# Attention with wide key chunks: three chunks of 128 keys and a shared rest of 64 instead of four chunks of 112, from unit 18 on

## The chip, the cores and the metric

The kernel runs on one core of one Trainium2 chip. The metric is the device time of one execution in microseconds (us). A NeuronCore has a matrix engine (TensorE, PE in the profile, its weight loads PEld), a vector engine (VectorE, DVE), a scalar engine (ScalarE, ACT), GpSimd (POOL), and SyncE (SP), which here issues the stores and the transposes by DMA. Each engine works through its own list of instructions in order and waits on semaphores where it needs another's result.

## The reference

Attention over 8 batches and 12 heads, 448 tokens each, head size 64, and behind it a two-layer network with a leaky ReLU:

```python
scores = scale * np.matmul(q, k.transpose(0, 1, 3, 2))
attn = softmax(scores)                       # over the 448 keys
attn_out = np.matmul(attn, v)                # (8, 12, 448, 64)
x = attn_out.transpose(0, 2, 1, 3).reshape(3584, 768)
h = x @ w_in                                 # 768 -> 2048
g = np.maximum(0.01 * h, h)
return (g @ w_out).astype(np.float32)        # 2048 -> 768
```

Inputs and output are float32; the products inside the kernel run in bfloat16. The kernel takes no maximum off the scores: it exponentiates the scaled scores directly, and divides by the sum afterwards.

## The kernel before, in words

**Units.** A unit is two heads of one batch: 48 units, six to a batch. For each unit q, k and v are loaded by DMA (converted to bfloat16 on the way), and copied by POOL into `qkb` (q and k side by side) and into `v_sb`, which holds a column of ones behind each head's 64 columns. q and k are then turned so that the head dimension lies on the partitions: `qkT`, with head 0 on partitions 0 to 63 and head 1 on 64 to 127. The first units are turned by PE, those from unit 15 on by a DMA transpose that SP issues (`dma_transposes`, L257).

**Scores.** The 448 keys are cut into four chunks of 112 (`SC`). A chunk is two matmuls of 448 columns (`scores`, L284), one for each head, each contracting the 64 rows of its half; they go to one PSUM slot of two banks. ACT exponentiates the slot in one instruction of 112 x 896 (`expo`, L296) into `e_sb`. Three such slots rotate. In the main part chunks come in bursts of three (`burst`, L819): six matmuls in a row, then three exponentials. A burst so covers three quarters of a unit.

**Rows.** When all of a unit's exponentials are there, `rows` (L790) multiplies them by v: for each of two heads, four groups of 112 queries and four key chunks one matmul of 65 columns, 32 in all; the 65th column is the sum of the exponentials. DVE takes the reciprocal of the sums and multiplies (L805, L806) into an x tile. `x_transposes` has SP turn the x tile by DMA into `xT`; for four units PE does it. The x tiles rotate over three buffers: the multiply of a unit must wait until the transpose of the unit three before has read its buffer.

**The network.** The 3584 tokens are cut into seven ranges (0, 640, 1152, 1664, 2176, 2688, 3072, 3584), numbered 0 to 6. For each range there are two stages. `hidden` computes the first layer in products of six matmuls (L489), in two chains with two PSUM banks each; ACT copies or DVE adds (L504, L516, L519) must empty a bank before the chain comes back to it. `second` computes the second layer from blocks of products of eight matmuls of 384 columns (L561), whose results DVE gathers into the tile o, which SP stores. Products are combined in a scheme that needs seven block products instead of eight, hence the many sums on DVE.

**The order of the work.** Everything is written in one program order, from which each engine takes its own instructions. Bursts and rows are put between the matmuls of `second` by `place` (L878), which keeps a small model of time (when PE is, when ACT will be through, when a slot will be free) and places a burst or the rows of a unit only when the model says that PE would not wait. `plan` (L875) says how many bursts go into each `second` stage: 9, 8, 8, 8, 8, 5, 0. In `hidden` there are no bursts, as two of the three slots serve the chains; rows of units that are ready are put in at every fourth step (L1001). At regular steps `advance` (L768) issues the loads (POOL), the casts (POOL) and the qkT transposes (SP) of later units. SP's list thus holds stores, qkT transposes and xT transposes in one order, and each waits for those ahead of it to be issued.

In the profile's time: `second` of range 0 runs from about 74 to 104 us, and then `hidden` and `second` of ranges 1 to 6 follow, with `hidden` from 104, 152.5, 201.5, 250, 298.5 and 341 us for ranges 1, 2, 3, 4, 5 and 6.

Of the kernel before, what the change touches and what calls it, by code (L numbers as in the profile page):

```python
# [16 lines left out]
def kernel(  # L17
# [9 lines left out]
    nc = tc.nc  # L27
# [9 lines left out]
    NW = DM // 2  # L37
    NU = B * HP
    scale = 1.0 / float(D) ** 0.5

# [8 lines left out]
    w_pool = ctx.enter_context(tc.tile_pool(name="weights", bufs=1))  # L49
    ld_pool = ctx.enter_context(tc.tile_pool(name="ld", bufs=2))  # L50
    cast_pool = ctx.enter_context(tc.tile_pool(name="cast", bufs=1))
# [30 lines left out]
    PL = D + 2  # L82
    v_sb = [v_pool.tile([SC, 2, NSC, VL], BF16, name=f"v{i}") for i in range(NV)]

    NE = 3
    EL = 2 * NSC * S
    e_sb = [exp_pool.tile([SC, EL + P - SC], BF16, name=f"e{i}") for i in range(NE)]


    NQ = 4  # L90
    QL = 2 * S
    qkT = [qk_pool.tile([P, QL + P - SC], BF16, name=f"qkT{i}") for i in range(NQ)]

# [25 lines left out]
    qk_sb = {}  # L119
    qkb = [cast_pool.tile([SC, 2, NSC, 2, D], BF16, name=f"qkb{i}") for i in range(4)]  # L120

# [3 lines left out]
    for t, n in ((h_mix, 2), (w_in_mix, 9), (w_mix, 9)):  # L125
        t = t.rearrange("p x k n -> p (x k n)")
        for j in range(n):
            rooms.append(t[:SC, ts(j, 4 * NSC * D)].bitcast(F32).rearrange("p (h so d) -> p h so d", h=2, so=NSC))

    def room(x):  # L130

        return rooms.pop(0) if rooms else ld_pool.tile([SC, 2, NSC, D], F32, name="f" + "qkv"[x])

    def half(t, i=None):

        t = t.rearrange("p h so d -> p (h so d)").bitcast(BF16)
        t = t.rearrange("p (u h so d) -> p u h so d", u=2, h=2, so=NSC)
        return t if i is None else t[:, i]

    def load_soft(u, n, which):  # L140
        b, hp = divmod(u, HP)
        for x in which:
            t = room(x)
            nc.gpsimd.dma_start(
                out=half(t)[:, :n].rearrange("p u h so d -> p (u h) (so d)"),
                in_=(q, k, v)[x][b, 2 * hp:2 * hp + 2 * n].rearrange(
                    "h (p so) d -> p h (so d)", so=NSC),
            )
            for i in range(n):
                raw.setdefault(u + i, {})[x] = half(t, i)  # L150

    def load_one(u, x, queue):
        b, hp = divmod(u, HP)
        t = room(x)
# [10 lines left out]
    def cast(u, parts=(0, 1, 2), by=nc.gpsimd.tensor_copy):  # L165
        if u >= NU:
            return
        for x in parts:
            f = raw[u].pop(x)
            if x < 2 and u not in qk_sb:  # L170
                qk_sb[u] = qkb[u % len(qkb)]
            t, n = (qk_sb[u][:, x], D) if x < 2 else (v_sb[u % NV], D)
            if f.dtype == BF16 and by == nc.gpsimd.tensor_copy:
                t, f, n = t.bitcast(F32), f.bitcast(F32), D // 2
            by(t.rearrange("p so h d -> p h so d") if x < 2 else t[:, :, :, :n], f)  # L175
    w_steps = []
# [59 lines left out]
    for t in e_sb:  # L236
        nc.vector.memset(t[:, EL:], 0.0)
    for t in qkT:
        nc.vector.memset(t[:, QL:], 0.0)
    fast = nc.vector.tensor_copy  # L240
# [12 lines left out]

    def turn(dst, src):
        nc.sync.dma_start_transpose(out=dst.rearrange("p (c s) -> p c s", s=SC), in_=src)
# [9 lines left out]
    def transposes(u, bank=None):  # L265
        if u >= min(NPE, NU):
            return
        for parts in ((1,), (0,)) if u == 0 else ((0, 1),):
            tr = turn_tile(bank)
            for i in parts:  # L270
                for so in range(NSC):
                    nc.tensor.transpose(  # L272
                        tr[:, i, ts(so, SC)], qk_sb[u][:, i, so], ident[:SC, :SC]
                    )
# [7 lines left out]
    sc_t = {}  # L282

    def scores(u, c):  # L284
        ps = next_slot()
        t = qkT[u % NQ]
        sc_t[u, c] = ps
        for j in range(2):
            nc.tensor.matmul(  # L289
                ps[:, j, :S],  # L290
                t[j * D:(j + 1) * D, S + c * SC:S + c * SC + P],
                t[j * D:(j + 1) * D, :S],
                start=True, stop=True,
            )

    def expo(u, c):  # L296
        e = e_sb[u % NE][:, :EL].rearrange("p (j c s) -> p j c s", j=2, c=NSC)
        nc.scalar.activation(e[:, :, c, :], sc_t.pop((u, c))[:SC, :, :S], AX.Exp, scale=scale)  # L298

    def pv(u, j, bank=None):  # L300
# [4 lines left out]
        for qc in range(NSC):  # L305
            for c in range(NSC):
                at = (j * NSC + c) * S + qc * SC
                nc.tensor.matmul(  # L308
                    ps[:, qc, :D + 1], e[:, at:at + P], vt[:, j, c, :D + 1],
                    start=(c == 0), stop=(c == NSC - 1),  # L310
# [452 lines left out]
    chunk = 4 * HP + 3  # L763
    rows_done = HP
    to = {"pe": HP + 2, "turn": NPE, "cast": HP + 4, "v": HP + 4, "load": [HP + 8] * 3}
# [24 lines left out]
    def rows():  # L790
# [3 lines left out]
        ps = next_slot()[:, :, :NSC * PL].rearrange("p j (q d) -> p j q d", q=NSC)  # L794
        for j in range(2):
            for qc in range(NSC):
                for c in range(NSC):
                    at = (j * NSC + c) * S + qc * SC
                    nc.tensor.matmul(  # L799
                        ps[:, j, qc, :D + 1], e[:, at:at + P], vt[:, j, c, :D + 1],  # L800
                        start=(c == 0), stop=(c == NSC - 1),
                    )
        x_t[u] = x_pool.tile([SC, NSC, 2, D], BF16, name="x")
        rec = r_pool.tile([SC, 2, NSC, 1], F32, name="rec")
        nc.vector.reciprocal(rec, ps[:SC, :, :, D:D + 1])  # L805
        nc.vector.tensor_mul(  # L806
            x_t[u].rearrange("p q j d -> p j q d"), ps[:SC, :, :, :D], rec.to_broadcast([SC, 2, NSC, D])
        )
        if u in X_PE:
# [9 lines left out]
    def burst(lazy=0):  # L819
        nonlocal chunk  # L820
        todo = [divmod(chunk + x, NSC) for x in range(3) if chunk + x < NU * NSC]
        assert rows_done > todo[-1][0] - NE and turned(todo[-1][0]) and to["v"] > rows_done
        for a, c in todo:
# [50 lines left out]

    plan = [9, 8, 8, 8, 8, 5, 0]  # L875
    model = {"now": 0.0, "act": 0.0, "free": {}, "ready": {}}

    def place(i, want, soon=0, full=True, calm=True, first=False, lazy=0, keen=NU, cap=NU):  # L878
# [3 lines left out]
        while True:  # L882
            settle_x(model["now"])
            now = model["now"]
            last = divmod(chunk + 2, NSC)[0]
            blocked = rows_done <= min(last, NU - 1) - NE
            u = rows_done
            whole = u < chunk // NSC
            at = [free.get(id(x), 0.0) for x in slots]
# [8 lines left out]
            if len(slots) < 3 and full and max(want, soon) > done and u <= min(last, NPE - 1) and state == 0:  # L898
# [4 lines left out]
                continue  # L903
            if want > done and state < 2 and turned(last) and not blocked and len(slots) == 3 and all(
                x <= now + 0.05 + 0.2 * j for j, x in enumerate(at)
# [8 lines left out]
                for x, t in enumerate(order[:chunk - start]):  # L914
                    model["act"] = max(model["act"], now + 0.45 + 0.2 * x) + 0.8
                    free[id(t)] = model["act"] + (0.3, 0.15 + 0.5 * (lazy > 1), 0.15 + 0.5 * lazy)[x]
                    if (start + x) % NSC == NSC - 1:
                        ready[(start + x) // NSC] = model["act"] + 0.1
                model["now"] = now + 0.78
                continue  # L920
            u = to["pe"]
            if first and full and state == 0 and u < min(NPE - 1, to["cast"] - 1) and u <= chunk // NSC + 1 and model["act"] <= now + 0.6:
# [4 lines left out]
                continue  # L927
            u = rows_done
            if calm and whole and not (lazy and late) and at[0] <= now + 0.05 and ready.get(u, 0) <= now + 0.05 and (
                u <= (chunk + 5) // NSC - NE or u < keen  # L930
            ) and u < cap:
# [9 lines left out]
    def second(i):  # L941
# [4 lines left out]
        for c in range(len(spots(i)[1])):  # L946
            for x, _ in enumerate(block_pair(i, c)):
                if x % 4 == 0:
                    advance(i + 1 < NR and rows_done >= need[i + 2] - 3 and not all(summed), (chunk + 3 * left - 1) // NSC)
                if c or x:  # L950
# [16 lines left out]
        assert left == 0 or chunk == NU * NSC, (i, left)  # L967
        assert i + 1 == NR or rows_done >= need[i + 2], (i, rows_done)
# [66 lines left out]
```

## Time and profile before

| | |
|---|---|
| time, median of 3 runs | 383.44 us (382.96 to 383.44) |
| the profiled execution | 382.9 us, span 381.1 us |
| granted PE clock | 1.0 throughout |
| busy: PE, ACT, DVE, POOL | 374.3, 265.1, 232.1, 111.7 us |
| exponentials, 112 x 896 (L298) | 192 of 920 ns |
| score matmuls, 64 x 448 (L289) | 384 |
| matmuls of rows (L799) | 1344 |
| transposes issued by SP | 33 of qkT (4.9 us to landing), 44 of xT (4.0 us) |
| loads of q, k, v issued by POOL | 19 each in the steady form, 6.0 to 8.9 us to landing |

Matmuls are pipelined and their lengths are modelled, so prices on PE are read as differences of starts. "L289" is line 289 of the kernel. In a tile's name the buffer number is left out: `sc` is any of the three slots, `g` one of the two banks. PEq, SPq and POOLq are the engines' sequencers, which issue DMAs.

### The profile page before, as it was taken

Reading aid. Unit: us, or ns where it says so; the run is one execution under the profiler, and the core shown is the slowest. Engines: PE = TensorE matmul, PEld = TensorE weight load, DVE = VectorE, ACT = ScalarE, POOL = GpSimd, SP = SyncE. Lnnn points to the kernel's source line nnn. Section 1 sums busy time; section 2 is a strip of 40 time slices with the busy share of each in tenths; the row PEclk is TensorE's granted clock in tenths of the full one; section 3 lists DMA queues with packets and bytes.
Section 4 is the critical chain, followed back from the end, with each engine's and each line's share of the span. In section 5 each row is a group of like instructions: output and inputs, shape, how many; then the busy total and the mean of one; then the engine's idle time right before and its main releaser. Section 6 shows DMA issues by size and latency. Waiting matters only on the chain.

```text
span 381.1 us, 10099 instructions
## 1 busy us (share of the span) xinstructions
PE 374.3 (98%) x4123; PEld 261.4 (69%) x4123; DVE 232.1 (61%) x510; ACT 265.1 (70%) x392; POOL 111.7 (29%) x223
## 2 busy tenths in 40 slices
PE   8899999999999999999999999999999999999996
PEld 6665658756598565986558865688656895668854
DVE  3662767776666645666466674665745665474753
ACT  6997885866768777588766777668777687717700
POOL 5966663452326211251121512213322000000000
PEclk9999999999999999999999999999999999999999
DMA  8999999999898945999458994679949630331023
GB/s 157 168 202 203 200 190 207 181 124 168 133 179 81 139 108 99 165 112 123 118 89 148 107 144 89 118 131 99 159 71 147 122 61 0 109 77 33 1 83 84
DMA packets 92798, 46.98 MB, mean 123 GB/s; under 512 B 51408, under 2 KB 89424, under 8 KB 92752
## 3 DMA queue, kind: packets, MB, share of 16 engines
q0 software_dynamic: 37536, 22.24, 45.6%
q1 hardware_dynamic: 54480, 23.44, 35.5%
q10 hardware_dynamic: 736, 0.66, 0.6%
q8 instruction: 32, 0.52, 0.6%
q14 instruction: 14, 0.11, 0.1%
HBM read 45.61 MB, written 11.01 MB: 149 GB/s over the span
## 4 chain that ended last, share of the span: by engine, by line
PE 94%; ACT 2%; DVE 2%; DMA 1%; issue 0%; DVEq 0%
PE g L561 34%; PE g L489 14%; PE sc L489 14%; PE sc L289 11%; PE sc L799 10%; PE g L370 4%; ACT e L298 2%; PE g L656 2%; PE g L272 1%; DMA hmix<-in_k_dram 1%; PE g L308 1%; PE sc L370 1%; DVE x L806 1%; PE g L335 0%; DVE qkT L278 0%
## 5 line engine op out<-in xcount | busy, mean ns | idle before, releaser
L298 ACT ACTIVATE e<-sc 112x896 bf16<-112x896 f32 x192 | 162.6, 920 | 45.2 <-PE sc L289 45.0
L561 PEld LDWEIGHTS <-h 128*128 128x128 bf16 x680 | 61.2, 98 | 48.0 <-issue 14.1
L561 PE MATMUL g<-w_out_sb,h 128*128 128x384 bf16 x448 | 87.2, 327 | 0.0
L478 ACT ACTIVATE h<-c 128x512 bf16<-128x512 f32 (+1 forms) x72 | 43.5, 611 | 24.0 <-DVE c L504 14.0
L489 PEld LDWEIGHTS <-w_in_sb 128*128 128x128 bf16 x576 | 54.3, 98 | 6.0
L289 PE MATMUL sc<-qkT 64*128 64x448 bf16 x384 | 50.0, 353 | 1.7 <-ACT e L298 0.6
L175 POOL COPY v<-fv 112x256 f32<-112x256 f32 x38 | 16.2, 425 | 117.3 <-PE sc L799 98.6
L799 PEld LDWEIGHTS <-e 112*128 112x128 bf16 x1344 | 46.5, 97 | 4.4
L799 PE MATMUL sc<-v,e 112*128 112x65 bf16 x1344 | 47.7, 193 | 0.0
L489 PEld LDWEIGHTS <-w_in_mix 128*128 128x128 bf16 x432 | 41.1, 98 | 4.1
L566 DVE COPY o<-g 128x384 f32<-128x384 f32 x53 | 29.4, 554 | 22.5 <-PE g L561 22.2
L561 PE MATMUL g<-w_mix,h 128*128 128x384 bf16 (+1 forms) x224 | 41.8, 325 | 0.0
L289 PEld LDWEIGHTS <-qkT 64*128 64x128 bf16 x384 | 15.8, 94 | 28.9 <-issue 19.6
L569 DVE TENSOR_TENSOR o<-o,g 128x384 f32<-128x384 f32 x42 | 23.2, 552 | 18.1 <-PE g L561 16.3
L805 DVE RECIPROCAL rec<-sc 112x8 f32<-112x8 f32 x42 | 8.7, 208 | 36.9 <-PE sc L799 36.7
L806 DVE TENSOR_TENSOR x<-sc,rec 112x512 bf16<-112x512 f32 x42 | 29.0, 691 | 1.5
L489 PE MATMUL g<-xT,w_in_sb 128*128 128x256 bf16 (+1 forms) x216 | 28.5, 268 | 0.0
L489 PE MATMUL sc<-xT,w_in_sb 128*128 128x256 bf16 (+1 forms) x216 | 28.5, 268 | 0.0
L175 POOL COPY qkb<-fq 112x256 f32<-112x256 f32 x38 | 16.7, 441 | 32.8 <-DMA fq<-in_q_dram 32.8
L175 POOL COPY qkb<-fk 112x256 f32<-112x256 f32 x38 | 17.4, 458 | 27.5 <-DMA fk<-in_k_dram 27.5
L561 PE MATMUL g<-w_mix,hmix 128*128 128x384 bf16 x112 | 21.7, 327 | 0.0
L489 PE MATMUL g<-x_mix,w_in_mix 128*128 128x256 bf16 (+1 forms) x144 | 19.0, 268 | 0.0
(107 smaller groups left out, 455.0 us busy)
## 6 DMA issues: line engine op xcount, KB each, us to landing
fq<-in_q_dram POOLq DMA_DIRECT2D x19, 224.0 KB, 7.5
fk<-in_k_dram POOLq DMA_DIRECT2D x19, 224.0 KB, 8.9
fv<-in_v_dram POOLq DMA_DIRECT2D x19, 224.0 KB, 6.0
w_in_sb<-in_moe_w_in_dram POOLq DMA_DIRECT2D x4, 768.0 KB, 12.2
w_out_sb<-in_moe_w_out_dram POOLq DMA_DIRECT2D x4, 768.0 KB, 17.9
out_dram<-o SPq DMA_DIRECT2D x7, 336.0 KB, 3.0
out_dram<-o SPq DMA_DIRECT2D x8, 288.0 KB, 3.3
out_dram<-o SPq DMA_DIRECT2D x7, 240.0 KB, 2.9
```

Source lines behind the costliest of these rows:

```text
L175: by(t.rearrange("p so h d -> p h so d") if x < 2 else t[:, :, :, :n], f)
L289: nc.tensor.matmul(ps[:, j, :S], t[j * D:(j + 1) * D, S + c * SC:S + c * SC + P], t[j * D:(j + 1) * D, :S], start=True, stop=True,)
L298: nc.scalar.activation(e[:, :, c, :], sc_t.pop((u, c))[:SC, :, :S], AX.Exp, scale=scale)
L370: nc.tensor.matmul(open_t[m][:, :n], w_in_sb[:, kk, ts(m, P)], xT[:, kk, at:at + n], start=(fresh and kk == kks[0]), stop=(kk == KD - 1),)
L478: nc.scalar.activation(hs[:, m:m + 2, cols], x.rearrange("p (m t) -> p m t", m=2), AX.Prelu, alpha=0.01)
L489: nc.tensor.matmul(ps[:, j * nh:(j + 1) * nh], w[:, kk, ts(j, P)], x[:, kk], start=(first and j == 0 and kk == 0), stop=(kk == KH - 1), sk ...
L561: nc.tensor.matmul(ps[:, cols], x[:, m], w[:, m], start=(first and m == 0), stop=(m == MH - 1), skip_group_check=True,)
L566: by(o[:, at], ps[:, :NW])
L569: nc.vector.tensor_add(o[:, at], o[:, at], ps[:, :NW])
L799: nc.tensor.matmul(ps[:, j, qc, :D + 1], e[:, at:at + P], vt[:, j, c, :D + 1], start=(c == 0), stop=(c == NSC - 1),)
L805: nc.vector.reciprocal(rec, ps[:SC, :, :, D:D + 1])
L806: nc.vector.tensor_mul(x_t[u].rearrange("p q j d -> p j q d"), ps[:SC, :, :, :D], rec.to_broadcast([SC, 2, NSC, D]))
```

## The change

From unit 18 on (`WIDE`, the first unit of batch 3) the 448 keys are cut into three chunks of 128 and a rest of 64.

- *Loads* (`load_wide`): k and v of two units come in three DMAs instead of one. One brings the 384 keys of the three chunks to 128 partitions; two bring the rests. Head 0's rest lies on partitions 0 to 63, head 1's on 64 to 127, and the other half of each head's place is set to zero once for each buffer. q is loaded as before.
- *Turning*: qkT of a unit holds 1024 columns (q with 112 of each 128 used, k three chunks and the rest) instead of 896. The rest is block diagonal: the keys of head 0 meet zeros in the rows of head 1, and the other way round.
- *Scores*: a burst is now one unit, three chunks of 128 keys, six matmuls. The rest (`rest`) is one matmul of 448 columns that contracts all 128 rows and serves both heads, and one exponential of 128 x 448. `place` puts it in after the burst, when a slot is free, and in `hidden` at a step where rows would stand.
- *Rows*: for each group of 112 queries six matmuls of 65 columns and one of 130 columns for the rest of both heads, 28 a unit instead of 32.
- *Buffers*: the x tiles rotate over two buffers instead of three, the multiply of a unit so waits for the transpose of the unit two before. The qkT tiles grow from 912 to 1024 columns.
- *Order*: `plan` becomes 8, 7, 6, 6, 6, 3, 0. A qkT transpose is issued for at most three units past the one being scored (four chunks' units past it before). In the built program `hidden` of ranges 2, 3, 4 and 5 now holds the rows of three units, at steps 2, 6 and 10, where it held two; `second` of these ranges holds correspondingly fewer. Copies of loaded data on POOL go as 32-bit words, as they did. On PE 150 matmuls and as many weight loads fall away; POOL issues 60 more DMAs and 20 more memsets.

```diff
+    WIDE = 3 * HP
+    NWC = S // P
+    REST = S - NWC * P
...
-    x_pool = ctx.enter_context(tc.tile_pool(name="x", bufs=3))
+    x_pool = ctx.enter_context(tc.tile_pool(name="x", bufs=2))
...
+    def load_wide(u, x):
+
+        b, hp = divmod(u, HP)
+        t = room(x).rearrange("p h so d -> p (h so d)").bitcast(BF16)
+        t = t.rearrange("p (u h so d) -> p u h so d", u=2, h=2, so=NSC)
+        src = (q, k, v)[x][b, 2 * hp:2 * hp + 4]
+        nc.gpsimd.dma_start(
+            out=t[:, :, :, :NWC].rearrange("p u h so d -> p (u h) (so d)"),
+            in_=src[:, :NWC * P].rearrange("h (p so) d -> p h (so d)", so=NWC),
+        )
+        for j in range(2):
+            own, other = (slice(y * REST, (y + 1) * REST) for y in (j, 1 - j))
+            if u < WIDE + 4:
+                nc.gpsimd.memset(t[other, :, j, NWC], 0.0)
+            nc.gpsimd.dma_start(out=t[own, :, j, NWC], in_=src[j::2, NWC * P:].rearrange("u r d -> r u d"))
...
     def dma_transposes(u):
         if NPE <= u < NU:
-            turn(qkT[u % NQ][:, :QL], qk_sb[u].rearrange("p i so h d -> p (i so h d)"))
+            rows_of, s = (P, P) if u >= WIDE else (SC, SC)
+            turn(qkT[u % NQ][:, :2 * NSC * s], qk_sb[u][:rows_of].rearrange("p so h d -> p (so h d)"), s)
...
     def expo(u, c):
-        e = e_sb[u % NE][:, :EL].rearrange("p (j c s) -> p j c s", j=2, c=NSC)
-        nc.scalar.activation(e[:, :, c, :], sc_t.pop((u, c))[:SC, :, :S], AX.Exp, scale=scale)
+        e = e_main(u)
+        nc.scalar.activation(e[:, :, c, :], sc_t.pop((u, c))[:e.shape[0], :, :S], AX.Exp, scale=scale)
+
+    def rest(u):
+
+        ps = next_slot()[:, 0, :S]
+        nc.tensor.matmul(ps, qkT[u % NQ][:, (2 * NSC - 1) * P:2 * NSC * P], q_of(u), start=True, stop=True)
+        at = 2 * NWC * S
+        nc.scalar.activation(e_sb[u % NE][:, at:at + S], ps, AX.Exp, scale=scale)
...
+        else:
             for qc in range(NSC):
+                b, y = divmod(2 * qc, NSC)
+                for j in range(2):
+                    for c in range(NWC):
+                        at = (j * NWC + c) * S + qc * SC
+                        nc.tensor.matmul(
+                            ps[:, b, y + j, :D + 1], e[:, at:at + P], vt[:, j, c, :D + 1],
+                            start=(y + j + c == 0), stop=False, skip_group_check=True,
+                        )
+                at = 2 * NWC * S + qc * SC
+                nc.tensor.matmul(
+                    ps[:, b, y:y + 2, :D + 1], e[:, at:at + P], vt[:, :, NWC, :D + 1],
+                    start=False, stop=True, skip_group_check=True,
+                )
...
-        if u < min(NU, chunk // NSC + NQ, to["cast"]) and (u <= due or not hold):
+        if u < min(NU, scored() + NQ - 1, to["cast"]) and (u <= due or not hold):
...
-    plan = [9, 8, 8, 8, 8, 5, 0]
+    plan = [8, 7, 6, 6, 6, 3, 0]
...
+            if calm and owed_rest and at[0] <= now + 0.05:
+                t = slots[0]
+                u = set_rest()
+                model["act"] = max(model["act"], now + 0.25) + 0.5
+                free[id(t)] = model["act"] + 0.15
+                ready[u] = model["act"] + 0.1
+                model["now"] = now + 0.19
+                continue
...
-            if step % 4 == 2 and (i > 1 or step > 2) and NSC * (rows_done + 1) <= chunk:
+            if step % 4 == 2 and owed_rest:
+                set_rest()
+            elif step % 4 == 2 and (i > 1 or step > 2) and rows_done < scored():
                 rows()
```

More of the change, by code (lines that the diff above doesn't have):

```diff
@@ L142, in load_soft @@
         for x in which:
+            if x > 0 and u >= WIDE:
+                load_wide(u, x)
+                continue
             t = room(x)
@@ L820, in burst @@
         nonlocal chunk
-        todo = [divmod(chunk + x, NSC) for x in range(3) if chunk + x < NU * NSC]
-        assert rows_done > todo[-1][0] - NE and turned(todo[-1][0]) and to["v"] > rows_done
+        todo = [at_chunk(chunk + x) for x in range(3) if chunk + x < total]
+        assert rows_done > todo[-1][0] - NE and turned(todo[-1][0]) and to["v"] > rows_done and not owed_rest
+        if todo[0][0] >= WIDE:
+            assert todo[0][1] == 0
+            owed_rest.append(todo[0][0])
         for a, c in todo:
@@ L903, in place @@
                 continue
-            if want > done and state < 2 and turned(last) and not blocked and len(slots) == 3 and all(
+            if want > done and state < 2 and turned(last) and not blocked and not owed_rest and len(slots) == 3 and all(
                 x <= now + 0.05 + 0.2 * j for j, x in enumerate(at)
@@ L921, in place @@
             u = to["pe"]
-            if first and full and state == 0 and u < min(NPE - 1, to["cast"] - 1) and u <= chunk // NSC + 1 and model["act"] <= now + 0.6:
+            if first and full and state == 0 and u < min(NPE - 1, to["cast"] - 1) and u <= scored() + 1 and model["act"] <= now + 0.6:
                 transposes(u)
@@ L948, in second @@
                 if x % 4 == 0:
-                    advance(i + 1 < NR and rows_done >= need[i + 2] - 3 and not all(summed), (chunk + 3 * left - 1) // NSC)
+                    advance(i + 1 < NR and rows_done >= need[i + 2] - 3 and not all(summed), at_chunk(chunk + 3 * left - 1)[0])
                 if c or x:
```

105 lines of the change are left out of this document (69 added, 36 removed).

## The prediction

> **What bounds the kernel now.** I read the page first: the engines' sums, the slices and the chain.
>
> ```profile
> PE 374.3 (98%) x4123; PEld 261.4 (69%) x4123; DVE 232.1 (61%) x510; ACT 265.1 (70%) x392; POOL 111.7 (29%) x223
> ...
> PE 94%; ACT 2%; DVE 2%; DMA 1%; issue 0%; DVEq 0%
> ```
>
> TensorE (PE) is busy 98% of the span and holds 94% of the chain, at full clock; ScalarE's (ACT) 70% lies beside it. The windows from 62 to 359 us show PE busy without a gap. So inside the stages that the change touches a microsecond saved on ACT is worth nothing, one saved on PE is worth itself, and any wait that reaches PE is paid in full. Next, prices: the PE timeline inside one `second` stage (start, length, line, count). Lengths are modelled, so I subtract starts.
>
> ```profile
> 140.87 1.14 PE L799 MATMUL sc<-v,e 112*128 112x65 bf16 x32
> 141.84 0.49 PE L561 MATMUL g<-w_out_sb,h 128*128 128x384 bf16 x2
> ...
> 144.90 1.15 PE L561 MATMUL g<-w_mix,h 128*128 128x384 bf16 x6
> 145.88 1.14 PE L561 MATMUL g<-w_out_sb,h 128*128 128x384 bf16 x6
> 146.96 0.74 PE L289 MATMUL sc<-qkT 64*128 64x448 bf16 x6
> 147.63 0.50 PE L561 MATMUL g<-w_out_sb,h 128*128 128x384 bf16 x2
> ```
>
> One unit's rows (32 matmuls of 65 columns) take 0.97 us, 30 ns each. Six matmuls of 384 columns take 0.98 us when rows of their own kind follow, but 1.08 when a burst follows: entering a burst costs 0.10. The burst takes 0.67, so 0.77 in all for six matmuls of 448 columns. These run in pairs: each contracts only 64 rows, the two heads lie on the two halves of the array, and a pair costs little more than one matmul.
>
> The third view decides the forecast: the timeline of one `hidden` stage, DVE and SP beside PE.
>
> ```profile
> 202.70 1.14 PE L799 MATMUL sc<-v,e 112*128 112x65 bf16 x32
> 203.23 4.99 SPq L255 DMA_TRANSPOSE qkT<-qkb  x3
> ...
> 204.19 0.69 DVE L806 TENSOR_TENSOR x<-sc,rec 112x512 bf16<-112x512 f32 x1
> ...
> 208.30 3.37 SPq L255 DMA_TRANSPOSE xT<-x  x2
> ...
> 209.89 0.82 PE L489 MATMUL g<-xT,w_in_mix 128*128 128x256 bf16 x6
> ...
> 210.77 0.68 DVE L519 TENSOR_TENSOR c<-c,g 128x512 f32<-128x512 f32 x1
> ...
> 212.51 0.82 PE L489 MATMUL g<-xT,w_in_sb 128*128 128x256 bf16 x6
> ```
>
> And, of the tile x in the window 208.2 to 208.5, the first of those two xT transposes:
>
> ```profile
> L255 SPq DMA_TRANSPOSE xT<-x x1: 1537/1537/1537, 208.3 to 208.3; - x1
> ...
> DMA to landing us min/median/max: 7.1/7.1/7.1
> ```
>
> DVE finished this unit's x at 204.9, but SP issues in order: three qkT transposes stood ahead, so the xT transpose left at 208.3 and landed at 215.4, 11.2 us after the multiply began. Now nobody minds, because the third x buffer is free.
>
> **The change, part by part.** The sum is made against the profiled execution, 382.9 us (span 381.1); the median of the runs, 383.44, is 0.5 above it.
>
> 1. *Bursts.* 30 units of four chunks were 40 bursts; they become 30. Ten bursts fewer: 10 x 0.77 = -7.7 us. Moving data now has a pitch of 128 with 112 used. No row shows such an operand; at worst the gaps cost columns, 512 instead of 448: three pairs x 64 columns at the 0.42 ns of a 448-column matmul (0.19 us, next item) is 0.08 us a unit, 2.4 in all; at best 0. I take 0: every kind of matmul in the views goes by the columns that it moves (65, 256, 384, 448 in 30, 109, 163, 190 ns), and the gaps are not moved.
>
> 2. *Rests.* 30 new matmuls of 128 x 448 at full height. The nearest row is `part` (L370), 448 columns: the chain in order of time has six of them last 1.14 us (at 35.04), 0.19 each, and 1.24 after a burst. 30 x 0.19 = +5.7. They have no partner on the other half of the array, so they save nothing against a pair of quarter chunks; only the entries saved in item 1 count. Bounds: 0.16 (a 384-column one) and 0.29 (with an entry as a burst has): +4.9 to +8.7.
>
> 3. *Rows.* 32 matmuls become 24 of 65 columns and 4 of 130. The columns stay 2080. 24 x 30 ns + 4 x 57 ns (two 27 ns of columns and the 3 ns that the 30 ns leave) = 0.95 instead of 0.97: -0.5 us over 30 units. [...]
>
> 4. *Exponentials.* Four of 920 ns (L298) become three and one of half length: some 0.4 us of ACT a unit. PE waits for ACT 0.6 us in the whole run ("PE sc L289 <- ACT e L298", twice), so this counts 0; its cover would have to go first.
>
> 5. *Loads and casts.* k and v of a pair of units come in three DMAs instead of one: 60 more issues on POOL at 0.70 us (L144), 42 us spread over some 200, and POOL stands idle 98.6 us for rows alone ("POOL v L175 <- PE sc L799"). Twenty small memsets and the same casts lie in that idle time too. The transfers shrink to 128 rows of 768 bytes and two blocks of 256-byte rows: 768 packets instead of 448 a load. Cost 0 as long as POOL is ahead; it shows in item 7.
>
> 6. *qkT transposes.* 1024 columns on 128 rows instead of 896: 1024 packets of 256 bytes for 896, 14% more. In a `second` stage the last one now follows the stores, as it did: it left at 189.2 and landed 4.5 us later, 20.6 into the stage, and the burst that reads it, by the prices above added over the new order, stands 21.4 in. With 14% more it still arrives. Cost 0, bound +0.5 in three stages.
>
> 7. *Two x buffers.* This is the new wait. In the built program `hidden` of ranges 2 to 5 now has the rows of three units, a, b, c, 24 matmuls apart, instead of two. The multiply that writes x of c waits for the xT transpose of a. That wait stands on DVE, in order; behind it are the sums c12 (L519), whose banks PE needs again at the next group of the stage.
>  In range 3 the rows of c fall at 209.89 (7.19 us after those of a at 202.70), so the multiply would start at 204.19 + 7.19 = 211.4; it must wait for 215.4: 4.0 us. Slack: the first L519 now ends at 212.7, and the next group on that bank starts at 212.51 + 0.97 = 213.5. PE stalls 4.0 - 0.8 = 3.2.
>  Range 4, same reading: multiply of a at 252.97, transposes issued 257.45, landing 7.3 later at 264.8; wait 4.6, stall 3.8.
>  Range 5 has shorter steps: multiply of a at 301.39, issue 306.08, landing 2.4 later; c wants to start at 307.05, waits 1.4, slack 0.55: stall 0.85.
>  Range 2: in the new order the xT transpose of a stands behind one qkT transpose, not three. The first one landed at 158.2 there; c's multiply comes at 162.6: no stall.
>  Sum +7.85. Lower bound 0 (the transposes land early, below). Upper: the three larger qkT ahead add 384 packets at 20 ns on 16 engines, 0.5 us a stage, and more load packets beside them perhaps 1: +4.5. I take the landings as they stand in the trace before, the nearest row there is, and leave the growth to the range.
>
> Sum: -7.7 + 5.7 - 0.5 + 7.85 = +5.4; 382.9 + 5.4 = **388.3 us**.
>
> **Rivals.**
>
> *A, the transposes land in time; faster.* Without item 7 the sum is -2.5, 380.4 us. It needs a's transpose to land by 212.2, within 3.9 us of its issue at 208.3. For it: the median over all 44 xT transposes is 4.0 us, and without loads beside it range 5 took 2.4. Against it: at just this place three stages show 7.1, 7.1 and 7.3, because POOL issues the q and k loads right after the rows of a, and the new order keeps that. [...] Chance 0.15.
>
> *B, the transfers become the bound.* If the smaller load packets cost as much as the 512-byte ones (76 ns in this window), a k load takes 320 x 76 ns / 16 = 1.5 us longer, x of a lands later by that in two stages, and the late qkT stalls the sixth burst: 388.3 + 3.0 + 1.5 = 392.8. Every fetch is two or three transfers ahead, which speaks against it. Chance 0.08.
>
> *C, only one stage pays in full.* The second qkT's delay is a matter of which load collides with it. If one of the two large stalls goes, the sum is +1.6 to +2.2, 384.5 to 385.1; if it goes and the rest halves, no change. Chance 0.20, of which 0.07 within 0.2% of before (0.77 us, about what a measurement here can tell).
>
> *Main case*, 386 to 391: 0.57.
>
> **How the numbers follow.** Faster 0.15 (A); same 0.07; slower 0.78 (main, B and the rest of C). The time is the main case's. The range leaves out most of A below and B above: 381.5 to 392.0; the main case's own range is 386 to 391.
>
> **What would show it.** Right: in ranges 3 and 4 the multiply that writes x waits 4 us or more for DMA, once a stage, and PE shows a gap of about 3 us after it in the products that follow; bursts at 0.77 and rests at 0.19; rows at 0.95; ACT busy some 11 us less with nothing gained. Wrong: no DVE wait for DMA in `hidden` (then A), or PE waiting for qkT in `second` (then B), or rests that cost 0.29.

## The result, and the profile after

The changed kernel takes 394.59 us (median of 4 runs, 393.19 to 398.36) beside 383.36 us for the kernel before: 1.0317 times as long, 95% interval 1.0254 to 1.038. The direction was forecast, the size was not: 388.3 us with a range of 381.5 to 392.0. A fifth run, 396.49 us, counts in the ratio and its interval but not in the median. The profiled execution of the changed kernel is the slowest of all, 398.36 us (span 396.2), against 382.9 us (span 381.1) before.

The page of the changed kernel, from its first, second and fourth parts:

```profile
PE 377.6 (95%) x3973; PEld 263.5 (66%) x3973; DVE 232.2 (59%) x513; ACT 253.4 (64%) x392; POOL 154.4 (39%) x303
...
PE   8899999999999996999999699998999999999996
...
PEclk9999999999999998999999899999999999999999
...
PE 71%; DMA 17%; DVE 4%; ACT 3%; issue 1%; SPq 1%; POOL 1%; DVEq 0%; POOLq 0%
```

PE now stands idle for two visible stretches (a 6 in slices 16 and 23 of 40, at 149 to 158 and 218 to 228 us), and DMA, which held 1% of the chain, holds 17%. Of these, 4% are qkT transposes and 3% xT transposes; most of the rest are two loads through which the chain passes in the start (w_out 6%, q 4%). ACT is busy 11.7 us less, as forecast, and nothing came of it. In the same two slices the granted clock shows an 8 where it was 9 throughout: that was in no part of the forecast.

Where the time went, stage by stage. Each number is the difference between the starts of the first product of this stage and of the next on PE, in the profiled executions; the last two columns belong to two experiments told of below.

| stage | before | after | turned at the rest | with the late fixes |
|---|---|---|---|---|
| start to `second` 0 | 73.04 | 73.97 | 73.19 | 73.16 |
| `second` 0 | 30.85 | 31.56 | 31.20 | 30.73 |
| `hidden` 1 | 20.29 | 20.26 | 20.27 | 20.27 |
| `second` 1 | 28.46 | **34.18** | 28.94 | 28.93 |
| `hidden` 2, `second` 2 | 20.29, 28.46 | 21.23, 27.51 | 21.23, 27.01 | 21.23, 27.01 |
| `hidden` 3, `second` 3 | 20.29, 28.49 | **26.86**, 27.06 | 21.23, 27.01 | 21.23, 27.12 |
| `hidden` 4, `second` 4 | 20.29, 28.46 | **23.24**, 27.17 | 21.23, 27.01 | 21.23, 27.14 |
| `hidden` 5, `second` 5 | 15.81, 26.00 | **17.99**, 24.77 | 16.75, 24.77 | 16.75, 24.08 |
| `hidden` 6 and `second` 6 | 40.39 | 40.45 | 40.27 | 40.33 |
| span | 381.12 | 396.24 | 380.10 | 379.21 |

Four stages carry the loss. What PE and DVE waited for, from the list of waits of the changed kernel (in all, times, longest, us):

```profile
DVE x L896 <- DMA xT<-x: 9.9, 4, 5.0
...
PE g L545 <- DVE c L575: 6.4, 3, 3.9
PEld L333 <- DMA qkT<-qkb: 5.1, 3, 3.8
PE sc L333 <- DMA qkT<-qkb: 3.9, 2, 3.4
```

The first two lines are the forecast's wait (item 7): the multiply that writes x waits for the transpose that reads the old x, and PE waits behind it for a sum of DVE. Three of the four waits for xT lie in `hidden` 3, 4 and 5 (4.97, 2.70 and 1.37 us); the fourth, 0.83 us at 48.36 in the start, was in no item. The other two lines are bursts that wait for their qkT, which item 6 had at nothing. Each is read from a timeline. First `hidden` 3, SP, PE, DVE (start, length, line, count):

```profile
210.02 0.34 PE L884 MATMUL sc<-v,e 128*128 128x65 bf16 x6
...
210.55 7.20 SPq L292 DMA_TRANSPOSE qkT<-qkb  x3
...
217.84 7.59 SPq L292 DMA_TRANSPOSE xT<-x  x3
...
223.53 0.69 DVE L896 TENSOR_TENSOR x<-sc,rec 112x512 bf16<-112x512 f32 x1 [4.97 <-DMA xT<-x]
224.14 0.68 DVE L575 TENSOR_TENSOR c<-c,g 128x512 f32<-128x512 f32 x1
...
224.87 1.44 PE L545 MATMUL g<-xT,w_in_sb 128*128 128x256 bf16 x6 [3.94 <-DVE c L575]
```

This is item 7 as it was drawn: unit a's x is ready at 212.18 (its multiply began at 211.49), but three qkT transposes stand ahead of its transpose on SP, so that leaves at 217.84 and lands 5.6 us later; c's multiply waits, the sum L575 waits behind it, and PE stands for 4.1 us. Six products of 256 columns then last 1.44 us, not 0.82. That is the clock. The windows of the changed kernel (us, busy time of each engine, granted clock, DMA share, GB/s):

```profile
core 0: us, PE busy (x) PEld busy (x) DVE busy (x) ACT busy (x) POOL busy (x), PEclk, DMA share, GB/s
148.46:152.23 3.77, 0.33 (x4) 0.01 (x2) 0.00 (x0) 0.45 (x2) 0.12 (x1) 1.00 1.42 183
152.94:156.35 3.41, 3.41 (x13) 1.55 (x12) 0.89 (x2) 2.83 (x4) 2.15 (x4) 0.50 0.56 64
...
224.62:228.03 3.41, 3.16 (x16) 2.17 (x16) 0.79 (x2) 2.94 (x6) 0.63 (x2) 0.50 1.21 120
274.57:276.51 1.94, 0.28 (x3) 0.10 (x1) 1.34 (x3) 0.02 (x1) 1.59 (x5) 1.00 0.20 43
276.60:280.01 3.41, 3.38 (x31) 2.87 (x31) 1.34 (x3) 3.14 (x7) 2.43 (x4) 1.00 0.87 93
```

At each of the two long waits the granted clock falls to 0.50 for 3.41 us, which costs about 1.7 us more (an estimate, 3.41 x 0.5); after the wait of `hidden` 4 (a gap of 1.94 us between starts) it does not. Then the surprise, `second` 1, SP and PE:

```profile
140.65 1.25 SPq L292 DMA_TRANSPOSE qkT<-qkb  x1
...
141.99 3.73 SPq L404 DMA_DIRECT2D out_dram<-o  x4
...
145.83 4.45 SPq L292 DMA_TRANSPOSE qkT<-qkb  x2
...
147.65 1.14 PE L617 MATMUL g<-w_out_sb,h 128*128 128x384 bf16 x6
...
152.23 0.74 PE L333 MATMUL sc<-qkT 64*128 64x448 bf16 x6 [3.44 <-DMA qkT<-qkb]
```

The sixth burst of this stage would have begun at 148.6. Its qkT left SP at 145.83, behind four stores, and landed at 152.18. In the kernel before, the qkT of the same unit stood ahead of the stores on SP, and left 11.3 us into the stage instead of 20.0:

```profile
135.48 1.24 SPq L255 DMA_TRANSPOSE qkT<-qkb  x1
...
139.90 1.99 SPq L348 DMA_DIRECT2D out_dram<-o  x4
```

The sum for the profiled execution: gaps of 3.6, 4.1, 1.8 and 1.0 us (3.77, 4.21, 1.94 and 1.09 between starts, less the 0.11 to 0.16 that a start takes anyhow) are 10.5; two halved windows 3.4; smaller gaps at 102, 202.5, 307 and 348 us together 2.4; the stretch before the first changed stage 0.9; the bursts, rests and rows -2.5 by the forecast's prices. That makes +14.7, and the span grew by 15.1. The other runs have no trace. Three of them (393.19 to 394.64) had a mean granted clock of 0.995 to 0.996 where the profiled one had 0.990, about what one halved window takes off instead of two (3.41 x 0.5 / 392 is 0.4%); the fifth (396.49) had 0.991, about two. So the median, 394.59, most likely holds one halved window, and the profiled execution two.

### The profile page after: what moved, and what is told of

Its sections match the earlier page's. It is cut to its first block, busy times and chain, and to the rows that moved or that the text cites. A ratio compares the mean times of both kernels' runs of the same rounds, so it can differ in the third digit from the quotient of the medians.

```text
span 396.2 us, 9887 instructions
## 1 busy us (share of the span) xinstructions
PE 377.6 (95%) x3973; PEld 263.5 (66%) x3973; DVE 232.2 (59%) x513; ACT 253.4 (64%) x392; POOL 154.4 (39%) x303
## 3 DMA queue, kind: packets, MB, share of 16 engines
q0 software_dynamic: 48096, 22.24, 49.1%
## 4 chain that ended last, share of the span: by engine, by line
PE 71%; DMA 17%; DVE 4%; ACT 3%; issue 1%; SPq 1%; POOL 1%; DVEq 0%; POOLq 0%
PE g L617 29%; PE g L545 12%; PE sc L545 12%; PE sc L333 6%; DMA w_out_sb<-in_moe_w_out_dram 6%; PE sc L884 5%; DMA qkT<-qkb 4%; DMA fq<-in_q_dram 4%; DMA xT<-x 3%; ACT e L347 2%; PE sc L889 2%; PE sc L873 1%; PE sc L352 1%; DVE x L896 1%; PE g L256 1%
## 5 line engine op out<-in xcount | busy, mean ns | idle before, releaser
L347 ACT ACTIVATE e<-sc 128x896 bf16<-128x896 f32 (+1 forms) x162 | 137.4, 922 | 48.8 <-PE sc L333 48.7
L617 PEld LDWEIGHTS <-h 128*128 128x128 bf16 x680 | 62.8, 98 | 50.9 <-issue 13.5
L207 POOL COPY v<-fv 128x256 f32<-128x256 f32 (+1 forms) x38 | 16.0, 422 | 100.6 <-PE sc L889 78.4
L333 PE MATMUL sc<-qkT 64*128 64x448 bf16 x324 | 42.9, 353 | 6.8 <-DMA qkT<-qkb 3.9
L896 DVE TENSOR_TENSOR x<-sc,rec 112x512 bf16<-112x512 f32 x42 | 29.0, 691 | 11.3 <-DMA xT<-x 9.9
L333 PEld LDWEIGHTS <-qkT 64*128 64x128 bf16 x324 | 12.8, 94 | 30.2 <-issue 17.9
L884 PEld LDWEIGHTS <-e 128*128 128x128 bf16 x720 | 30.4, 97 | 3.5 <-ACT e L347 2.3
L884 PE MATMUL sc<-v,e 128*128 128x65 bf16 x720 | 32.1, 193 | 0.0
L207 POOL COPY qkb<-fk 128x256 f32<-128x256 f32 (+1 forms) x38 | 18.1, 478 | 24.3 <-DMA fk<-in_k_dram 24.3
L889 PE MATMUL sc<-v,e 128*128 128x130 bf16 x120 | 26.7, 223 | 0.0
L617 PE MATMUL g<-w_mix,hmix 128*128 128x384 bf16 x112 | 24.5, 339 | 0.0
```

The source lines that it names most:

```text
L333: nc.tensor.matmul(ps[:, j, :S], t[j * D:(j + 1) * D, k0:k0 + P], q_of(u)[j * D:(j + 1) * D] if u >= WIDE else t[j * D:(j + 1) * D, :S], s ...
L347: nc.scalar.activation(e[:, :, c, :], sc_t.pop((u, c))[:e.shape[0], :, :S], AX.Exp, scale=scale)
L617: nc.tensor.matmul(ps[:, cols], x[:, m], w[:, m], start=(first and m == 0), stop=(m == MH - 1), skip_group_check=True,)
L884: nc.tensor.matmul(ps[:, b, y + j, :D + 1], e[:, at:at + P], vt[:, j, c, :D + 1], start=(y + j + c == 0), stop=False, skip_group_check=True,)
L889: nc.tensor.matmul(ps[:, b, y:y + 2, :D + 1], e[:, at:at + P], vt[:, :, NWC, :D + 1], start=False, stop=True, skip_group_check=True,)
L896: nc.vector.tensor_mul(x, ps[:SC, :, :, :D], rec.to_broadcast([SC, 2, NSC, D]))
```

## The experiments

The theory at this point: the work itself saves 2.5 us, and all of the loss comes from the order on SP's queue, which two x buffers make visible in `hidden` and the missing lead of the qkT transposes in `second` 1. Its rivals: the third x buffer alone is what is missing; the smaller load packets slow the transposes (B); ACT's saved time is worth something, or nothing.

**A third x buffer.** From unit 21 on, every third unit's x lies in a tail of the first `e_sb` buffer, which grows by 64 columns for it; the order of the work stays.

```diff
-    e_sb = [exp_pool.tile([P, EL + P - SC], BF16, name=f"e{i}") for i in range(NE)]
+    e_sb = [exp_pool.tile([P, EL + P - SC + (D if i == 0 else 0)], BF16, name=f"e{i}") for i in range(NE)]
+    X_LAST = (2 * NWC + 1) * S + P - SC
...
-        x_t[u] = x_pool.tile([SC, NSC, 2, D], BF16, name="x")
+        if u > WIDE + 2 and u % 3 == 2:
+            x_t[u] = e_sb[0][:SC, X_LAST:X_LAST + NSC * 2 * D].rearrange("p (q j d) -> p q j d", q=NSC, j=2)
+        else:
+            x_t[u] = x_pool.tile([SC, NSC, 2, D], BF16, name="x")
```

> The changed kernel with a third x buffer again, from unit 21 on (every third unit's x tile lies in a tail of 512 columns behind the shortened exponentials of one e buffer; the order of the work is kept). Theory (buffer): the DVE waits for xT in hidden of ranges 3, 4 and 5, 6.9 us of PE stall in the profile and 1.7 us of halved clock after the longest, go away: 394.6 - 8.6, that is 385 to 388 us, with no gap over 1 us left in hidden, while the 3.8 us wait for a qkT transpose in second of range 1 stays. Rival (transfers are the bound): the waits only move, to qkT or to the banks, and the time stays above 391 us.

Measured: 387.06 us (385.94 to 387.83), 1.0097 times before (1.0072 to 1.0122). The `hidden` stages fall to 21.23, 21.23 and 16.75 us; `second` 1 stays at 34.12 with the same gap (3.98 us) and the same halved window behind it:

```profile
147.30:151.30 4.00, 0.36 (x3) 0.00 (x0) 0.00 (x0) 0.49 (x2) 0.00 (x0) 0.96 1.41 173
151.00:154.41 3.41, 3.09 (x12) 1.17 (x13) 0.89 (x2) 2.44 (x3) 2.99 (x6) 0.50 0.51 92
```

So the buffer accounts for all of the `hidden` waits, and for none of the one in `second` 1. Two of the four runs of this kernel, 385.94 and 386.68 us, had a mean clock of 1.0, which leaves no room for a halved window; the other two, 387.45 and 387.83 us, had 0.994 and 0.996.

**The next qkT turned at the rest.** Two x buffers again; a qkT transpose is issued behind each rest, the moment at which its buffer can be had.

```diff
         u = owed_rest.pop(0)
         rest(u)
+        n = to["turn"]
+        if n < min(NU, scored() + NQ - 1, to["cast"]):
+            dma_transposes(n)
+            to["turn"] += 1
         return u
```

> The changed kernel with two x buffers, but the next qkT transpose is issued directly behind each rest, where it becomes allowed, and so ahead of the stores of the first pair of blocks on SP's list. Theory (queue order): the 3.8 us wait in second of range 1 and the halved clock after it (1.7 us) go, and the smaller waits for qkT in ranges 2 and 4; the waits for x in hidden stay: 388 to 391 us. Rival (transfers are the bound): the transposes land as late as before, 393 to 396 us.

Measured: 383.12 us (381.88 to 383.86), 0.9991 times before (0.9976 to 1.0006); the expectation was 5 us too high. It was to mend `second` 1 and the smaller waits for qkT alone, and it mended the waits for x as well. `second` 1 is 28.94 us: the qkT of the sixth burst leaves at 140.54 instead of 145.83. And in `hidden` the waits for x are gone without a third buffer. SP of this kernel, that qkT first and then the stretch around the start of `hidden` 3 (201.83):

```profile
140.54 1.31 SPq L292 DMA_TRANSPOSE qkT<-qkb  x1
...
196.79 2.18 SPq L292 DMA_TRANSPOSE qkT<-qkb  x1
201.31 2.24 SPq L404 DMA_DIRECT2D out_dram<-o  x4
205.33 8.73 SPq L292 DMA_TRANSPOSE xT<-x  x3
214.17 1.25 SPq L292 DMA_TRANSPOSE qkT<-qkb  x1
```

The three qkT transposes that stood ahead of xT now leave inside `second` 2. The xT of unit a leaves as soon as its x is ready, at 205.33 (the multiply began at 204.6), and lands after 5.5 us, in time. The profiled execution is the fastest of the ten (381.88 us); why the median lies 1.2 us above it is not shown.

**Both.** The order of the last one and the third buffer.

> Both at once: third x buffer and the qkT transpose directly behind the rest. Theory: what is left of the change is its work on PE, -2.5 us by the prices in the prediction, and half a microsecond of small waits: 380.5 to 382.5 us, below the kernel before. Rival (transfers are the bound): 60 more loads in smaller packets and 14% larger transposes keep it above 385 us.

Measured: 383.16 us (382.05 to 384.01), 0.9998 times before (0.9986 to 1.001), which is no gain over two buffers. With the order mended, the buffer is worth nothing; the expectation had added up two cures of one disease. A gap of 1.06 us in `second` 1 (30.01 us there) is most of what sets its profile apart: a burst again waits for its qkT, 0.74 us, so in this stage the mended order has little to spare.

**Before, with two x buffers.** `bufs=3` of the x pool becomes 2 in the kernel before, nothing else.

> The kernel before with two x buffers instead of three, nothing else. Theory (the buffer costs only where three units' rows stand in one hidden stage): before has two there, the multiply after next comes 20 us later, so no change, 383.0 to 384.5 us. Rival (two buffers are too few by themselves): waits of 3 to 4 us in several ranges, 388 us or more.

Measured: 384.06 us (383.10 to 385.33), 1.0016 times before (1.0002 to 1.003). Two buffers by themselves cost 0.7 us. All four `hidden` stages stay at 20.29, 20.29, 20.29 and 15.81 us. The profiled execution, the slowest of the ten, lost nearly all of its time before range 1, and part of it to the missing third buffer: in the start the third multiply (48.49 us) waits for xT, and PE behind it, where with three buffers nothing waits. From its list of waits (in all, times, longest, us):

```profile
DVE x L806 <- DMA xT<-x: 1.0, 1, 1.0
...
PE sc L289 <- DVE x L806: 0.4, 1, 0.4
```

The changed kernel has the same wait (0.83 us at 48.36). What hurts it most, though, is two buffers together with the rows of three units in one `hidden` stage and a late xT.

**xT ahead of the qkT.** The changed kernel with its two buffers; in the first three steps of `hidden` no qkT transpose is issued.

```diff
-    def advance(hold=False, due=NU):
+    def advance(hold=False, due=NU, turning=True):
...
-        if u < min(NU, scored() + NQ - 1, to["cast"]) and (u <= due or not hold):
+        if turning and u < min(NU, scored() + NQ - 1, to["cast"]) and (u <= due or not hold):
...
-            advance()
+            advance(turning=step > 2)
```

> The changed kernel with two x buffers, where in hidden no qkT transpose is issued in the first three steps, so that on SP's list the xT transpose of the first of the three units stands ahead of the three qkT transposes instead of behind them. Nothing else moves on PE. Theory (the wait for the x buffer is made by SP's order): the waits in hidden go as with a third buffer, 385 to 388 us, and the 3.8 us wait in second of range 1 stays. Rival (two buffers are too few at this spacing, or the transposes are slow whatever stands ahead): hidden of range 3 stays 3 us or more too long, 391 us and up.

Measured: 386.56 us (385.42 to 388.38), 1.0059 times before (1.0039 to 1.0079). SP in `hidden` 3:

```profile
211.45 1.21 SPq L292 DMA_TRANSPOSE xT<-x  x1
212.76 5.68 SPq L292 DMA_TRANSPOSE qkT<-qkb  x3
218.53 3.57 SPq L292 DMA_TRANSPOSE xT<-x  x2
```

The same transposes, one moved to the front, and the three `hidden` stages are at 21.23, 21.23 and 16.75 us, as with a third buffer. `second` 1 keeps its gap (4.08 us, 34.39 in all). Together with the third x buffer and the transposes turned at the rest, this shows that in `hidden` the order on SP makes the waits for x; the buffer count only decides whether they are felt.

**Loads of before in three pieces.** The kernel before, k and v loads from unit 18 on as three DMAs each, the short one in two parts.

```diff
...
+            if x > 0 and u >= 3 * HP:
+                nc.gpsimd.dma_start(out=o[:, :, :3], in_=src[:, :, :3])
+                for j in range(2):
+                    own = slice(64 * j, 64 + 48 * j)
+                    nc.gpsimd.dma_start(out=o[own, :, 3], in_=src[own, :, 3])
...
```

> The kernel before, but the k and v loads from unit 18 on come in three DMAs each, to the same places: 384-byte and 128-byte writes, 896 packets a load instead of 448, 60 more issues on POOL. Theory (loads are fetched ahead and cost nothing): 383 to 384.5 us. Rival (transfers are the bound): they alone cost 3 us or more, 386 us and up, with PE or POOL waiting for fk and fv.

Measured: 383.17 us (382.80 to 384.51), 0.9996 times before (0.9984 to 1.0007). The loads' queue, from the pages of before and of this kernel (packets, MB, share of 16 engines):

```profile
q0 software_dynamic: 37536, 22.24, 45.6%
```

```profile
q0 software_dynamic: 51936, 22.24, 52.1%
```

14400 packets more, even more than the change adds (48096 in all), and no time. Nor is a third x buffer hiding a delay: the first xT transposes of `hidden` 2, 3 and 4 landed after 7.6, 7.1 and 7.2 us here, and after 7.1, 7.1 and 7.3 us in the kernel before. So rival B, in which the smaller packets make x land 1.5 us later, falls.

**Two fixes.** In the mended order two gaps remain: 1.06 us at 100.9, where a burst in `second` 0 needs the bank that PE's own transposes of unit 17 used, and 0.86 us at 332.4 in `second` 5, where the rows come just before a product whose bank DVE has not emptied. So the planner's estimate for such a bank goes from 1.0 to 1.6 us, and no rows are placed at the fourth step of a block pair.

```diff
-            model["free"][id(slots[0])] = model["now"] + 1.0
+            model["free"][id(slots[0])] = model["now"] + 1.6
...
-            if calm and whole and not (lazy and late) and at[0] <= now + 0.05 and ready.get(u, 0) <= now + 0.05 and (
+            if calm and room_for_rows and whole and not (lazy and late) and at[0] <= now + 0.05 and ready.get(u, 0) <= now + 0.05 and (
...
-                left -= place(i, left, calm=x not in (1, 2), keen=need[min(i + 2, NR)], cap=NU if all(summed) else need[i + 2])
+                left -= place(i, left, calm=x not in (1, 2), keen=need[min(i + 2, NR)], cap=NU if all(summed) else need[i + 2], room_for_rows=x != 3)
```

> The kernel of e2 (qkT transposes directly behind the rest, two x buffers) with two small waits removed by place: the last burst of range 0 stands four matmuls later behind the PE transposes of unit 17 (0.7 us waited there for a copy on DVE), and no unit's rows stand at the fourth step of a pair of blocks (0.7 us in range 5, where DVE emptied a bank late). Theory (only PE work is left): 1.4 us below e2, 381 to 382 us, below the kernel before by 0.3 to 0.7%. Rival (what e2 lacks of the 2.5 us lies in waits that vary from run to run, not in these two): 382.5 to 383.5, no difference from before.

Measured: 384.40 us (383.09 to 385.04), 1.0021 times before (1.0007 to 1.0035), slower than without the fixes. Both gaps closed (`second` 0 from 31.20 to 30.60, `second` 5 from 24.77 to 24.08), but the start grew from 73.19 to 75.38 us. The 1.6 us also holds for three units that PE transposes early, before the first `second` stage, and there PE, of this kernel, now waits:

```profile
61.71 0.50 PE L712 MATMUL g<-xT,w_in_sb 128*128 128x192 bf16 x4
63.17 1.48 PE L712 MATMUL g<-xT,w_in_sb 128*128 128x192 bf16 x16 [0.96 <-DVE xT L392]
...
65.33 0.49 PE L712 MATMUL g<-xT,w_in_sb 128*128 128x192 bf16 x4 [0.48 <-DVE xT L392]
```

In the profiled executions 1.3 us are gained and 2.2 lost.

**The rest's exponential twice.** On top of the last one, each rest's exponential is done a second time, into the same place: some 17 us of ACT put back (30 of 0.56; the busy time of ACT rises by 15.1).

```diff
         nc.scalar.activation(e_sb[u % NE][:, at:at + S], ps, AX.Exp, scale=scale)
+        nc.scalar.activation(e_sb[u % NE][:, at:at + S], ps, AX.Exp, scale=scale)
```

> The kernel of e5 with the exponential of each rest done twice into the same place, so that ACT gets back what the change saves it: 30 times some 0.45 us, 13 us more of ACT busy. Theory (ACT lies beside PE and its saving was worth nothing): within 1 us of e5. Rival (ACT's relief is what lets the new order run without waits): 2 us or more above e5, with PE waiting for L354.

Measured: 388.71 us (387.64 to 390.39), 1.014 times before (1.0115 to 1.0166), 4.3 us more than the kernel it was added to. The theory, less than 1 us, falls. PE of this kernel:

```profile
PE sc L333 <- ACT e L355: 1.7, 8, 0.2
...
PE sc L894 <- ACT e L355: 0.9, 5, 0.2
```

Bursts in the new order come as close as 3.25 us apart, and their exponentials with the rest's take 2.54 + 0.56 = 3.1 us of ACT. Another 0.56 does not fit, and the slot comes late; the time is lost in `second` 1 to 5, where bursts stand. So what ACT saves is worth no time, as item 4 says, but it is not free either: at this pace four exponentials of 0.92 us, 3.7 us a unit, would not fit either (worked out, not run).

**The late fixes only.** The order that turns qkT at the rest, no rows at the fourth step, and the 1.6 us for unit 17 alone, which leaves the early units as they were.

```diff
-            model["free"][id(slots[0])] = model["now"] + 1.6
+            model["free"][id(slots[0])] = model["now"] + (1.6 if owed_x[0][0] == 3 * HP - 1 else 1.0)
```

> The version of e2 (next qkT transpose issued behind the rest, two x buffers), with the planner's estimate for a bank with PE transposes raised from 1.0 to 1.6 us for unit 17 alone, and no rows at the fourth step of a block pair. Theory (the changed kernel's own work saves 2.5 us, and e2 lost 0.7 in second of range 0 and 0.7 in second of range 5 to late banks; e5's late start came from the earlier units alone): start at 73.2 as in e2, second of range 0 30.6, second of range 5 24.1, span 378.7 to 379.2, median 381.3 to 382.2, faster than before by 0.3 to 0.6%. Rival (these gaps only move, as the 1.6 us of e5 moved them): a gap of 0.5 us or more opens at another place, span 380 or more, ratio 0.998 to 1.001.

Measured: 381.85 us (380.77 to 382.73), 0.9964 times before (0.9947 to 0.9981). Faster than both kernels: 12.7 us below the changed kernel, 1.4 below before. From its page:

```profile
PE 372.8 (98%) x3973; PEld 261.8 (69%) x3973; DVE 233.3 (62%) x513; ACT 253.1 (67%) x392; POOL 154.2 (41%) x303
...
PEclk9999999999999999999999999999999999999999
...
PE 94%; ACT 2%; DVE 2%; issue 0%; DVEq 0%
```

The chain is PE's again, the clock is whole, and between 20 us and the end no two starts on PE lie more than 0.45 us apart. The span of 379.2 us is 1.9 us below the span of before, where the prices of bursts, rests and rows promised 2.5.

## Why the prediction was wrong

Direction and main mechanism held. The size did not, and it failed at three steps: a stage was left out of item 6, the landings in item 7 were mis-sized, and the sum had no term for a slower clock. In the profiled execution the forecast's +5.4 us becomes +14.7 by +3.6 (item 6 in `second` 1), +3.4 (two halved windows), -0.95 (item 7), +2.4 (four smaller gaps) and +0.9 (the start); the last two were in no item.

- *Item 6 failed.* "Cost 0, bound +0.5 in three stages" was worked out for a stage of six bursts, and there it nearly held: in `second` 2 the last qkT left 16.8 us into the stage (16.2 in the trace before) and landed after 5.2 us, and ranges 2 to 4 lost 0.7 us together. `second` 1 has seven bursts and was left out. Its sixth needs a qkT that SP issues only after the stores, 20.0 us into the stage, and that took 6.35 us to land: 3.6 us of stall, and 1.7 of halved clock behind it. The turned-at-the-rest order, which issues that transpose 5.3 us earlier (4.1 earlier within the stage), ends the wait; a third x buffer or xT ahead of qkT does not.
- *Item 7 held as a mechanism; its terms were off.* Ranges 3, 4, 5 were put at 3.2, 3.8 and 0.85 us and cost 4.1, 1.8 and 1.0: 6.9 for 7.85. The landings were taken from the trace before (7.1 and 7.3 us for xT) and were 5.6 and 4.4, while xT left later after its multiply than before (6.35 us in range 3 instead of 4.1, 5.3 in range 4 instead of 4.5), since three qkT took SP 7.2 and 6.3 us. From the multiply to the landing that makes 11.9 us for 11.2 in range 3 and 9.7 for 11.8 in range 4: the errors nearly cancel in the one and not in the other. Range 2 was rightly at nothing. The upper bound put 20 ns on a transpose's packet; of the 46592 packets of 256 bytes on that queue, the packet records of the trace before show a median of 18 ns and a mean of 32.
- *A term was missing.* The sum paid a stall at its length. In the profiled execution the two longest cost about 1.7 us each on top, an estimate from the granted clock of 0.50 for 3.41 us. What starts such a stretch no run shows: the two here start at 152.94 and 224.62 us, the first 0.71 us after PE had started again, the second 0.25 us before (see the last section).
- *Items 1 to 3 held*, within 0.01 us a unit. From the timeline of PE of the changed kernel in `second` 2:

```profile
191.58 0.49 PE L617 MATMUL g<-w_out_sb,h 128*128 128x384 bf16 x2
192.00 0.74 PE L333 MATMUL sc<-qkT 64*128 64x448 bf16 x6
192.68 1.15 PE L617 MATMUL g<-w_out_sb,h 128*128 128x384 bf16 x6
193.66 0.35 PE L352 MATMUL sc<-qkT 128*128 128x448 bf16 x1
193.85 1.46 PE L617 MATMUL g<-w_mix,h 128*128 128x384 bf16 x8
```

 The two products ahead of the burst take 0.42 us (0.10 of it the entry), the burst 0.68 (0.67 before, at 146.96), a rest 0.19, with no entry of its own; the pitch of 128 costs no more than that 0.01. The rows of a unit go from 0.97 to 0.96 us, where 0.95 was put. In ranges 2 to 4 an undisturbed pair of stages (that of the turned-at-the-rest order) goes from 48.75 to 48.24 us, -0.51; the items give -2 x 0.77 + 6 x 0.19 - 6 x 0.02 = -0.52.
- *Item 4 held as a price, not as a reason.* ACT's time does lie beside PE, but the doubled exponential shows less than 0.6 us a unit of room in the new order, not the ample cover that the 0.6 us of waits before suggested.
- *Item 5 held* as far as it was tried: the split loads cost nothing in the kernel before.
- *The rivals.* A did not come: in ranges 3 and 4 the xT transposes landed in 5.6 and 4.4 us where A needed 3.9, and they left later. B's time, 392.8, is the nearest to the result, and it did name the burst that waits, but by luck: its mechanism fell with the split loads, and an earlier place in SP's order was enough to end the wait. C came in part: range 4 paid half.

Open: of the 0.9 us that the start took longer in the profiled execution, the wait for xT at 48.36 makes about half (a gap of 0.62 us on PE); the multiply of the unit two before it, at 39.85 us instead of 39.41, is already 0.4 us late, and why is not shown. Open too is why the qkT of `second` 1 took 6.35 us to land where the one 5.2 us before it took 3.05, with which it would have landed at 148.9 and cost 0.3 us instead of 3.6. The k loads that POOL issued at 144.98 and 145.72 lie beside the later one; no run here takes them away.

## What to carry to other kernels

Where one queue issues several kinds of transfers in order, go through that list for each stage before a buffer is given up: the slack of a buffer is that of the transfer that frees it, with all that stands ahead of it, and a stage that differs from its neighbours by one burst wants its own check. A short reordering of the queue (issue a transfer where its own input and buffer become free, not at a fixed step) brought back nearly all that two buffers seemed to cost. And a change of an estimate in a planner has to be looked at wherever the estimate is used, as the early units showed.

## What the runs showed of the hardware

A long PE stall can cost more than its length. In the traces, gaps of 3.8 to 4.2 us between starts each came with 3.41 us at a granted clock of 0.50, at or behind their end (twice in the changed kernel, once with a third x buffer, once with xT ahead of qkT), and gaps of 1.94 us and less with none; sizes between these did not occur. In the changed kernel the first halved window began 0.71 us after PE had started again (152.94 and 152.23), the second 0.25 us before it did (224.62 and 224.87). The extra cost is not sure to come: two of the four runs with a third x buffer and four of the six with xT ahead had a mean clock of 0.998 or more, where one halved window takes off 0.4%. These runs have no trace.

Smaller packets cost no time here: 14400 more on the loads' queue, for the same 22.24 MB, raised its share from 45.6% to 52.1% of the engines, and the time stayed within 0.2%.
